# Splitting two of the down projection's seven block products a second time

## The chip, the cores and the metric

The kernel runs on one core of one Trainium2 chip. The metric is device time in microseconds (us) of one execution. Shorter is better.

## The reference

The reference mixes a sliding-window attention block `a` and a gated MLP block `b` with a sigmoid gate per token:

```
x = A_x                                     # 2048 tokens, 1024 features, bf16
g = sigmoid((x * gate_w).sum(-1))
a = attention(x @ wqkv, 32 heads, window 8, dilation 2) @ wo
b = (gelu(x @ w_gate) * (x @ w_up)) @ w_down        # 3584 hidden features
out = g * a + (1 - g) * b
```

The last step of both blocks is a matrix product, with `wo` (1024 x 1024) and with `w_down` (3584 x 1024). The kernel scales the attention output by `g` and the MLP's hidden values by `1 - g`, puts them side by side along the contraction, and so has one product for both: 2048 tokens by 4608 contracted features by 1024 outputs. That product is called `down`, and the change lies in it alone.

## The kernel before

Everything up to `down` (the gate and up products, q, k and v, the windowed softmax and the weighted sum of v) is unchanged and fills the first 522 us of the span. It leaves the hidden values in `h_d` and the attention output in `o_d`, both in device memory.

`down(s)` runs twice, for token halves `s` = 0 and 1 (1024 tokens each). In each call the left operand is cut into four blocks A11, A12, A21, A22 and the right one into R11, R12, R21, R22. The first index of an R block and the second of an A block run over the contraction (2304 features each, which are `NK` = 18 slots of 128), the others over tokens or outputs (512 each). A block is a buffer of 18 x 512 bf16 values per partition; ten such buffers, `bufs`, hold all blocks. The four output blocks are made from seven block products instead of eight, in Winograd's form of Strassen's scheme. One block product is 72 matmuls of 128 x 128 weights by 512 columns: four groups `j` of 128 tokens by 18 slots, written out by `mm`. In order they are

1. A11 x R11 into the four banks XP (its copy is kept in `u2`),
2. A12 x R21 on top of it in XP, which is output block (0, 0),
3. S x T1 into the four banks VP (copy kept in `qs`), with S = A21 + A22 and T1 = R12 - R11,
4. S x T2 into XP, with S now A21 + A22 - A11 and T2 = R22 - T1; it is added to `u2`, and that to `qs`,
5. A12 x R22 on top of VP, with A12 now A12 - S; plus `u2` it is output block (0, 1),
6. A11 x R12 into XP, with A11 now A11 - A21 and R12 now R22 - R12; plus `qs` it is output block (1, 1),
7. A22 x R21 on top of XP, with R21 now R21 - T2; plus `u2` it is output block (1, 0).

The sums and differences of blocks are VectorE's: `comb_task` makes one in five instructions over 4, 4, 4, 4 and 2 slots, `scale_task` multiplies the 14 slots of hidden values of an A block by `1 - g` in four instructions, and S - A11 goes in four pieces, one per `j`. ScalarE copies banks out. Output tiles are 128 x 512: `add_out` adds on VectorE from a bank into one of four small output tiles (`R_OUT`), and `emit` stores it, by GpSimd's DMA queue for s = 0 and by SyncE's for s = 1. The loads of the second half's blocks (`loads_1` to `loads_6`) are issued on SyncE's queue between the products of the first half.

The order on each engine is the order in which the program writes the instructions (`manual_schedule`); `take(rest, k)` writes k pieces of pending VectorE work between two groups of a product, `run(rest)` all that is left. The framework adds the semaphore waits.

Of the kernel before, what the change touches and what calls it, by code (L numbers as in the profile page):

```python
# [9 lines left out]
ALU = mybir.AluOpType  # L10
# [5 lines left out]
P = 128  # L16
SC = 512
# [37 lines left out]
R_BUF = tuple(9 + 18 * k for k in range(10))  # L55
R_U2 = 0
R_QS = 189
R_OUT = (8, 197, 198, 199)
KV = AC + HALO


# [5 lines left out]
def kernel(  # L67
# [12 lines left out]
    nc = tc.nc  # L80
    Bsz, S, D = A_x.shape
# [8 lines left out]
    NK = NPAIR + NT // 2  # L90
# [10 lines left out]
    def reg(kb, n):  # L101
        o = int(kb * KB)
        return arena[:, o:o + n]

    def reg3(kb, a, b):
        return reg(kb, a * b).rearrange("p (a b) -> p a b", a=a)
# [4 lines left out]
    def regf(kb, n):  # L111
        return reg(kb, 2 * n).bitcast(F32)

    banks = psum.tile([P, 8, SC], F32, tag="banks", bufs=1, name="banks")

    def bank(i):
        return banks[:, i, :]
# [8 lines left out]
    V = nc.vector  # L126
    TT = V.tensor_tensor

    with tc.manual_schedule(engines={mybir.EngineType.PE, mybir.EngineType.DVE, mybir.EngineType.Activation,
# [42 lines left out]
        for s in range(2):  # L172
            b0 = R_X[s]
            f = XF()
# [10 lines left out]
        def flat(a):  # L185
            return a.rearrange("p a b -> p (a b)")
# [353 lines left out]
        prod = [reg3(o, NWIN, AC) for o in pr_off]  # L540
# [210 lines left out]
        NH_ = NPAIR  # L751

        def load_A(b, s, half, c, i0, i1, with_o):
            t0 = s * SUP + c * SC
            nc.sync.dma_start(out=b[:, i0:i1, :], in_=h_src(half, t0, i0, i1))
            if with_o:
                nc.sync.dma_start(out=b[:, NH_:NK, :], in_=o_d[:, half * 4:half * 4 + 4, t0:t0 + SC])

        def h_src(half, t0, i0, i1):
            return h_d[:, :, t0:t0 + SC].rearrange("p (i two) s -> p i two s", two=2)[:, i0:i1, half, :]  # L760

        def load_R(b, half, nh):
            n0 = nh * SC
            nc.sync.dma_start(out=b[:, 0:NH_, :],
                              in_=B_w_down[:, n0:n0 + SC].rearrange("(i two p) n -> p i two n", two=2, p=P)[:, :, half, :])
            nc.sync.dma_start(out=b[:, NH_:NK, :],
                              in_=A_wo[:, n0:n0 + SC].rearrange("(p t) n -> p t n", t=NT)[:, 4 * half:4 * half + 4, :])
# [4 lines left out]
        qs = regf(R_QS, 4 * SC).rearrange("p (j n) -> p j n", j=4)  # L772
        on = [0]

        def out_tile():
            k = on[0] % 4
            on[0] += 1
            return reg(R_OUT[k], SC)

# [3 lines left out]
        def Bs(s):  # L783
            return {k: bufs[v] for k, v in plan[s].items()}

        def scale_task(b, s, c, ia, ib):
            t0 = s * SUP + c * SC
            om = omgrep[:, t0:t0 + SC].rearrange("p (o s) -> p o s", o=1)
            for i0 in range(ia, ib, 4):
                i1 = min(i0 + 4, ib)  # L790
                TT(out=b[:, i0:i1, :], in0=b[:, i0:i1, :], in1=om.to_broadcast([P, i1 - i0, SC]), op=ALU.mult)  # L791
                yield 0.05 + 0.273 * (i1 - i0)

        def comb_task(o_, a, b, op, step=4):
            for i0 in range(0, NK, step):
                i1 = min(NK, i0 + step)
                f = lambda t_: flat(t_[:, i0:i1, :])
                TT(out=f(o_), in0=f(a), in1=f(b), op=op)  # L798
                yield 0.05 + 0.273 * (i1 - i0)

        def run(*gens):
            for g in gens:
                for _ in g:
                    pass

        def pieces(*gens):
            for g in gens:
                yield from g

        def take(g, k):  # L810
            for _ in range(k):
                if next(g, None) is None:
                    break
# [19 lines left out]
        def loads_1(s):  # L833
            B = Bs(s)
            load_A(B["A11"], s, 0, 0, 0, NH_, True)
            load_R(B["R11"], 0, 0)

        def loads_2(s):
            B = Bs(s)
            load_A(B["A12"], s, 1, 0, 0, NH_, True)  # L840
            load_R(B["R21"], 1, 0)

        def loads_3(s):
            load_A(Bs(s)["A21"], s, 0, 1, 0, NH_, True)

        def loads_4(s):
            load_A(Bs(s)["A22"], s, 1, 1, 0, NH_, True)

        def loads_5(s):
            load_R(Bs(s)["R12"], 0, 1)  # L850

        def loads_6(s):
            load_R(Bs(s)["R22"], 1, 1)

        def down(s):
            B = Bs(s)
            last = s == 1
            eng = nc.sync if last else nc.gpsimd
            base = s * SUP
            XT, VT = (6, 7, 0, 1), (5, 2, 3, 4)  # L860

            def mm(ps, L, R, j, start):
                for q, i in enumerate(KORD):
                    nc.tensor.matmul(ps, lhsT=L[:, i, j * P:(j + 1) * P], rhs=R[:, i, :], start=(start and q == 0),  # L864
                                     stop=(q == NK - 1), skip_group_check=not start)

            def emit(ot, c, nh, j):
                r0 = base + c * SC + j * P
                eng.dma_start(out=o2[r0:r0 + P, nh * SC:(nh + 1) * SC], in_=ot)

            def add_out(ps, t_, c, nh, j):
                ot = out_tile()
                TT(out=ot, in0=ps, in1=t_, op=ALU.add)  # L873
                emit(ot, c, nh, j)

            A11, A12, A21, A22 = B["A11"], B["A12"], B["A21"], B["A22"]
            R11, R12, R21, R22, S, T2 = B["R11"], B["R12"], B["R21"], B["R22"], B["S"], B["T2"]
            T1 = R11
            XP = [bank(XT[j]) for j in range(4)]
            VP = [bank(VT[j]) for j in range(4)]  # L880
            rest = pieces(scale_task(A21, s, 1, 0, NH_), scale_task(A22, s, 1, 0, NH_), comb_task(S, A21, A22, ALU.add))
            for j in range(4):
                mm(XP[j], A11, R11, j, True)
                nc.scalar.copy(out=u2[:, j, :], in_=XP[j])  # L884
                yield
                take(rest, 3)
            run(rest)
            rest = comb_task(T1, R12, R11, ALU.subtract)
            for j in range(4):
                mm(XP[j], A12, R21, j, False)  # L890
                ot = out_tile()
                nc.scalar.copy(out=ot, in_=XP[j])
                emit(ot, 0, 0, j)
            run(rest)
            t2 = comb_task(T2, R22, T1, ALU.subtract)
            for j in range(4):
                mm(VP[j], S, T1, j, True)
                nc.scalar.copy(out=qs[:, j, :], in_=VP[j])
            run(t2)
            for j in range(4):  # L900
                js = slice(j * P, (j + 1) * P)
                TT(out=S[:, :, js], in0=S[:, :, js], in1=A11[:, :, js], op=ALU.subtract)  # L902
            run(comb_task(A12, A12, S, ALU.subtract), comb_task(A11, A11, A21, ALU.subtract))
            if not last:
                loads_1(1)
            rest = pieces(comb_task(R12, R22, R12, ALU.subtract), comb_task(R21, R21, T2, ALU.subtract))
            for j in range(4):
                mm(XP[j], S, T2, j, True)
                TT(out=u2[:, j, :], in0=XP[j], in1=u2[:, j, :], op=ALU.add)
                TT(out=qs[:, j, :], in0=qs[:, j, :], in1=u2[:, j, :], op=ALU.add)  # L910
                take(rest, 2)
            for j in range(4):
                mm(VP[j], A12, R22, j, False)
                add_out(VP[j], u2[:, j, :], 0, 1, j)
                take(rest, 1)
            run(rest)
            if not last:
                loads_2(1)
                loads_3(1)
                loads_5(1)  # L920
                rest = pieces(scale_task(Bs(1)["A11"], 1, 0, 0, NH_), scale_task(Bs(1)["A12"], 1, 0, 0, NH_))
            for j in range(4):
                mm(XP[j], A11, R12, j, True)
                add_out(XP[j], qs[:, j, :], 1, 1, j)
                take(rest, 1)
            if not last:
                loads_4(1)
                loads_6(1)
            for j in range(4):
                mm(XP[j], A22, R21, j, False)  # L930
                add_out(XP[j], u2[:, j, :], 1, 0, j)
                take(rest, 1)
            run(rest)

        n = len(units)
# [78 lines left out]
```

## Time and profile before

| | us |
|---|---|
| median of 3 runs | 745.09 (745.02 to 745.28) |
| the profiled execution | 744.98 |
| its span from first to last instruction | 743.2 |
| outside the span | 1.8 |

| engine | busy us | share of the span |
|---|---|---|
| TensorE (PE) | 730.6 | 98% |
| VectorE (DVE) | 594.8 | 80% |
| ScalarE (ACT) | 290.6 | 39% |
| GpSimd (POOL) | 74.4 | 10% |

A row of the profile names a line, an engine, an operation and its tiles; behind it stand how often it ran, its busy time and the mean of one. Busy times of neighbours overlap by some 0.1 us, so what a queue of equal instructions takes is read from the timeline, which merges neighbours into one row with a start and a length. The time in brackets at the end of a timeline row is the idle time of the engine before it, with what ended it. In the source of before, line 864 is the matmul of `mm`, 791 `scale_task`, 798 `comb_task`, 902 the pieces of S - A11, 909 and 910 the additions to `u2` and `qs`, 873 `add_out`, 884, 892 and 898 ScalarE's copies, 869 the stores.

### The profile page before, as it was taken

What the parts mean: (1) busy time and instruction counts of PE and PEld (TensorE: products, weight loads), DVE (VectorE), ACT (ScalarE), POOL (GpSimd) and SP (SyncE); (2) the same over time, 40 slices, a digit from 0 to 9 for tenths busy, and PEclk for the clock granted to TensorE, in tenths of its full rate; (3) what the DMA queues carried; (4) which work ended last, traced back from release to release, by engine and by line L of the source; (5) the groups of instructions that cost most, each with busy time, mean ns of one, the idle gap of its engine ahead of it and who ended that gap; (6) DMA issues with size and microseconds to landing.
All of it is one profiled execution on the core that took longest, in us unless ns stands there. A gap on an engine that the chain in (4) does not pass through costs nothing.

```text
span 743.2 us, 9134 instructions
## 1 busy us (share of the span) xinstructions
PE 730.6 (98%) x3497; PEld 356.3 (48%) x3567; DVE 594.8 (80%) x644; ACT 290.6 (39%) x498; POOL 74.4 (10%) x128
## 2 busy tenths in 40 slices
PE   8999999999999999999999999999999999999998
PEld 4465566555544444444444444444444444444443
DVE  3958888967999999999999999984487954936921
ACT  4454445535466655555555555555111000110000
POOL 1011111221201010101010010000010021000000
PEclk9999999999999999999999999999999999999999
DMA  9960000272323625535345644447990799400011
GB/s 279 267 202 24 19 15 22 75 227 95 106 81 108 194 77 185 181 104 160 128 142 171 212 145 142 154 159 264 291 307 1 246 360 359 138 28 1 9 42 36
DMA packets 107213, 106.95 MB, mean 144 GB/s; under 512 B 16656, under 2 KB 94480, under 8 KB 107168
## 3 DMA queue, kind: packets, MB, share of 16 engines
q1 hardware_dynamic: 97856, 77.41, 34.0%
q0 software_dynamic: 9024, 28.42, 11.4%
q8 instruction: 28, 0.46, 0.2%
q10 hardware_dynamic: 288, 0.52, 0.2%
q14 instruction: 17, 0.14, 0.1%
HBM read 73.73 MB, written 30.51 MB: 140 GB/s over the span
## 4 chain that ended last, share of the span: by engine, by line
PE 68%; issue 12%; DVE 4%; POOL 1%; DMA 1%; ACT 0%; DVEq 0%; POOLq 0%
PE banks L329 38%; PE banks L864 29%; PE banks L565 1%; DVE arena L366 1%; DVE arena L285 1%; POOL h_d L247 1%; DVE arena L560 1%; DVE arena L607 0%; DMA h_d<-arena 0%; DMA arena<-h_d 0%; POOL o_d L710 0%; DVE arena L246 0%; DVE md L633 0%; ACT L641 0%; DVE md L644 0%
## 5 line engine op out<-in xcount | busy, mean ns | idle before, releaser
L329 PE MATMUL banks<-arena 128*128 128x512 bf16 x2135 | 474.1, 379 | 4.2 <-DVE arena L366 1.3
L329 PEld LDWEIGHTS <-arena 128*128 128x128 bf16 x2184 | 239.9, 111 | 236.9 <-issue 11.1
L864 PE MATMUL banks<-arena 128*128 128x512 bf16 x989 | 217.1, 379 | 1.9 <-DVE arena L791 0.9
L864 PEld LDWEIGHTS <-arena 128*128 128x128 bf16 x1008 | 98.6, 98 | 120.0 <-DVE arena L791 1.3
L366 DVE TENSOR_TENSOR arena<-banks,arena 128x1024 bf16<-128x1024 f32 x78 | 95.2, 1221 | 45.9 <-PE banks L329 27.4
L352 ACT COPY arena<-banks 128x512 f32<-128x512 f32 x78 | 45.7, 586 | 130.2 <-PE banks L329 130.2
L683 DVE TENSOR_TENSOR arena<-arena 128x2048 bf16<-128x2048 bf16 x64 | 77.0, 1220 | 0.4
L337 ACT CAST arena<-banks 128x512 bf16<-128x512 f32 x102 | 59.7, 585 | 44.6 <-PE banks L329 44.3
L560 DVE TENSOR_TENSOR arena<-arena 128x2048 bf16<-128x2048 bf16 x64 | 75.2, 1219 | 0.3
L690 DVE TENSOR_TENSOR arena<-arena 128x2048 bf16<-128x2048 bf16 (+2 forms) x96 | 73.8, 776 | 1.0
L798 DVE TENSOR_TENSOR arena<-arena 128x2048 bf16<-128x2048 bf16 (+1 forms) x70 | 73.3, 1111 | 0.1
L873 DVE TENSOR_TENSOR arena<-banks,arena 128x512 bf16<-128x512 f32 x24 | 16.6, 690 | 47.0 <-PE banks L864 41.7
L359 ACT COPY banks<-banks 128x512 f32<-128x512 f32 x78 | 44.5, 571 | 21.7 <-PE banks L329 19.8
L347 ACT COPY banks<-banks 128x512 f32<-128x512 f32 x78 | 45.0, 577 | 14.2 <-PE banks L329 13.4
L247 POOL DMA_DIRECT2D h_d<-arena x28 | 20.0, 715 | 288.6 <-DVE arena L246 275.3
L791 DVE TENSOR_TENSOR arena<-arena,omgrep 128x2048 bf16<-128x2048 bf16 (+1 forms) x32 | 33.2, 1085 | 11.3 <-DMA arena<-h_d 11.2
L884 ACT COPY arena<-banks 128x512 f32<-128x512 f32 x8 | 4.7, 586 | 90.3 <-PE banks L864 90.3
L285 DVE TENSOR_TENSOR arena<-arena 128x1024 bf16<-128x1024 bf16 x60 | 38.6, 685 | 0.5
L335 ACT ACTIVATE arena<-banks 128x512 bf16<-128x512 f32 x54 | 32.2, 597 | 15.3 <-PE banks L329 15.2
L246 DVE TENSOR_TENSOR arena<-arena 128x2048 bf16<-128x2048 bf16 x28 | 34.1, 1216 | 1.7 <-ACT arena L337 1.5
L374 ACT ACTIVATE arena<-arena 128x1024 bf16<-128x1024 bf16 x27 | 28.3, 1048 | 0.0
L902 DVE TENSOR_TENSOR arena<-arena 128x2304 bf16<-128x2304 bf16 x8 | 10.8, 1357 | 21.7 <-PE banks L864 21.7
(68 smaller groups left out, 245.6 us busy)
## 6 DMA issues: line engine op xcount, KB each, us to landing
h_d<-arena POOLq DMA_DIRECT2D x28, 512.0 KB, 4.1
arena<-in_B_w_down_dram SPq DMA_DIRECT2D x8, 1792.0 KB, 13.2
arena<-h_d SPq DMA_DIRECT2D x6, 1792.0 KB, 13.6
arena<-in_B_w_gate_dram SPq DMA_DIRECT2D x15, 512.0 KB, 5.2
arena<-in_B_w_up_dram SPq DMA_DIRECT2D x15, 512.0 KB, 4.4
arena<-in_A_wqkv_dram SPq DMA_DIRECT2D x6, 1024.0 KB, 10.3
arena<-v_d SPq DMA_DIRECT2D x8, 544.0 KB, 6.3
v_d<-arena POOLq DMA_DIRECT2D x16, 256.0 KB, 2.3
```

Of the source, the lines that this page charges most:

```text
L285: TT(out=o_, in0=a, in1=b_, op=op)
L329: self.pe = nc.tensor.matmul(ps, lhsT=self.L[form](kt), rhs=rhs[:, kt, :], start=(start and kt == 0), stop=(kt == HK - 1), skip_group_chec ...
L337: nc.scalar.copy(out=o_, in_=i_)
L347: nc.scalar.copy(out=self.Y, in_=self.X)
L352: nc.scalar.copy(out=self.p5s, in_=self.V)
L359: nc.scalar.copy(out=self.Z, in_=self.Y)
L366: TT(out=self.T[:, :, c2s], in0=pair, in1=self.p5s.rearrange("p (o n) -> p o n", o=1).to_broadcast([P, 2, SC]), op=ALU.add)
L560: TT(out=dst, in0=q.rearrange("p (o s) -> p o s", o=1).to_broadcast([P, NWIN, AC]), in1=_win_ap(k, [[-DIL, NWIN], [1, AC]]), op=ALU.mult)
L683: TT(out=prod2[(t // 2) % 2][:, t % 2], in0=ab, in1=_win_ap(v[:, t, HALO:HALO + AC], [[SJ, NJ], [-DIL, NWIN], [1, SJ]]), op=ALU.mult)
L690: TT(out=out_, in0=h(0), in1=h(1), op=ALU.add)
L798: TT(out=f(o_), in0=f(a), in1=f(b), op=op)
L864: nc.tensor.matmul(ps, lhsT=L[:, i, j * P:(j + 1) * P], rhs=R[:, i, :], start=(start and q == 0), stop=(q == NK - 1), skip_group_check=not ...
```

## The change

Products 4 (S x T2) and 6 (A11 x R12) are each cut once more by the same scheme (`level2`). A block becomes four quarters of 9 slots by 256 columns (`quarter`), and the product seven inner ones, each of 2 groups by 9 slots of matmuls with 256 columns, 18 in all. `forms_L` and `forms_R` make the four quarter forms that each operand needs on VectorE, one instruction of 2304 elements each. The inner sums stay in the two halves of the four XP banks: VectorE zeroes the left halves (`zero_left`), ScalarE copies half banks into one another between the inner products, and two VectorE instructions add the copy `p5d` of the third inner product at the end.

The quarter forms need room. `LF` lies in the buffer of R11, `RF2` in that of A22, `RF7` in that of S. So A22 is loaded and scaled a second time for product 7. The copy `p5d` takes two of the four output tiles, which leaves two. Several steps move: R12 becomes R22 - R12 ahead of T2 instead of during product 4; A12 - S and A11 - A21 are no longer written together; `woven` alternates the left and right forms during product 5; R21 - T2 and A22's second scaling follow `level2` of product 6, and the four `add_out` of product 6 follow them; the second half's loads are written in another order, and the scaling of its A12 moves from product 6 of the first half to product 1 of the second.

```diff
@@ -55,7 +55,8 @@
 R_BUF = tuple(9 + 18 * k for k in range(10))
 R_U2 = 0
 R_QS = 189
-R_OUT = (8, 197, 198, 199)
+R_OUT = (8, 197)
+R_P5D = 198
 KV = AC + HALO
 
 
@@ -773,7 +774,7 @@
         on = [0]
 
         def out_tile():
-            k = on[0] % 4
+            k = on[0] % 2
             on[0] += 1
             return reg(R_OUT[k], SC)
 
@@ -852,6 +853,61 @@
         def loads_6(s):
             load_R(Bs(s)["R22"], 1, 1)
 
+        KH, HN = NK // 2, SC // 2
+        p5d = regf(R_P5D, SC).rearrange("p (j n) -> p j n", j=2)
+
+        def quarter(b, kh, h):
+            return b[:, kh * KH:(kh + 1) * KH, h * HN:(h + 1) * HN]
+
+        def quads(b):
+            return b.rearrange("p k n -> p (k n)").rearrange("p (f k n) -> p f k n", f=4, k=KH)
+
+        def forms_L(f, b):
+            q = lambda kh, h: quarter(b, kh, h)
+            for o_, a, b_, op in ((f[:, 0], q(0, 1), q(1, 1), ALU.add), (f[:, 1], f[:, 0], q(0, 0), ALU.subtract),
+                                  (f[:, 2], q(0, 0), q(0, 1), ALU.subtract), (f[:, 3], q(1, 0), f[:, 1], ALU.subtract)):
+                TT(out=o_, in0=a, in1=b_, op=op)
+                yield 1.3
+
+        def forms_R(f, b):
+            q = lambda kh, h: quarter(b, kh, h)
+            for o_, a, b_, op in ((f[:, 0], q(0, 1), q(0, 0), ALU.subtract), (f[:, 1], q(1, 1), f[:, 0], ALU.subtract),
+                                  (f[:, 2], q(1, 1), q(0, 1), ALU.subtract), (f[:, 3], q(1, 0), f[:, 1], ALU.subtract)):
+                TT(out=o_, in0=a, in1=b_, op=op)
+                yield 1.3
+
+        def woven(*gens):
+            for cs in zip(*gens):
+                yield from cs
+
+        def zero_left(b0, b1):
+            for b in (b0, b1):
+                V.memset(banks[:, b:b + 2, 0:HN], 0.0)
+
+        def level2(b0, b1, L, R, lf, rf):
+            lq, rq = lambda r, c: quarter(L, c, r), lambda r, c: quarter(R, r, c)
+            c = lambda i, h, j: banks[:, (b0, b1)[i] + j, h * HN:(h + 1) * HN]
+            both = lambda i, h: banks[:, (b0, b1)[i]:(b0, b1)[i] + 2, h * HN:(h + 1) * HN]
+
+            def prod(i, h, l, r, then=None):
+                for j in range(2):
+                    for kt in range(KH):
+                        nc.tensor.matmul(c(i, h, j), lhsT=l[:, kt, j * P:(j + 1) * P], rhs=r[:, kt, :], start=False,
+                                         stop=(kt == KH - 1), skip_group_check=True)
+                    if then:
+                        then(j)
+
+            cp = lambda d, s_: nc.scalar.copy(out=d, in_=s_)
+            prod(0, 0, lq(0, 0), rq(0, 0), lambda j: cp(c(1, 1, j), c(0, 0, j)))
+            prod(0, 0, lq(0, 1), rq(1, 0))
+            prod(1, 0, lf[:, 0], rf[:, 0], lambda j: cp(p5d[:, j, :], c(1, 0, j)))
+            prod(1, 1, lf[:, 1], rf[:, 1], lambda j: cp(c(0, 1, j), c(1, 1, j)))
+            prod(1, 1, lf[:, 2], rf[:, 2], lambda j: cp(c(1, 0, j), c(1, 1, j)))
+            prod(0, 1, lf[:, 3], rq(1, 1))
+            TT(out=both(1, 1), in0=both(1, 1), in1=p5d, op=ALU.add)
+            prod(1, 0, lq(1, 1), rf[:, 3])
+            TT(out=both(0, 1), in0=both(0, 1), in1=p5d, op=ALU.add)
+
         def down(s):
             B = Bs(s)
             last = s == 1
@@ -878,54 +934,61 @@
             T1 = R11
             XP = [bank(XT[j]) for j in range(4)]
             VP = [bank(VT[j]) for j in range(4)]
-            rest = pieces(scale_task(A21, s, 1, 0, NH_), scale_task(A22, s, 1, 0, NH_), comb_task(S, A21, A22, ALU.add))
+            LF, RF2, RF7 = quads(R11), quads(A22), quads(S)
+            rest = pieces(scale_task(A12, s, 0, 0, NH_) if last else (), scale_task(A21, s, 1, 0, NH_),
+                          scale_task(A22, s, 1, 0, NH_), comb_task(S, A21, A22, ALU.add))
             for j in range(4):
                 mm(XP[j], A11, R11, j, True)
                 nc.scalar.copy(out=u2[:, j, :], in_=XP[j])
                 yield
                 take(rest, 3)
             run(rest)
-            rest = comb_task(T1, R12, R11, ALU.subtract)
             for j in range(4):
                 mm(XP[j], A12, R21, j, False)
                 ot = out_tile()
                 nc.scalar.copy(out=ot, in_=XP[j])
                 emit(ot, 0, 0, j)
-            run(rest)
-            t2 = comb_task(T2, R22, T1, ALU.subtract)
+            run(comb_task(T1, R12, R11, ALU.subtract), comb_task(R12, R22, R12, ALU.subtract))
             for j in range(4):
                 mm(VP[j], S, T1, j, True)
                 nc.scalar.copy(out=qs[:, j, :], in_=VP[j])
-            run(t2)
+            run(comb_task(T2, R22, T1, ALU.subtract))
+            zero_left(XT[0], XT[2])
+            run(forms_R(RF2, T2))
             for j in range(4):
                 js = slice(j * P, (j + 1) * P)
                 TT(out=S[:, :, js], in0=S[:, :, js], in1=A11[:, :, js], op=ALU.subtract)
-            run(comb_task(A12, A12, S, ALU.subtract), comb_task(A11, A11, A21, ALU.subtract))
-            if not last:
-                loads_1(1)
-            rest = pieces(comb_task(R12, R22, R12, ALU.subtract), comb_task(R21, R21, T2, ALU.subtract))
+            run(forms_L(LF, S), comb_task(A12, A12, S, ALU.subtract))
+            level2(XT[0], XT[2], S, T2, LF, RF2)
+            load_A(A22, s, 1, 1, 0, NH_, True)
             for j in range(4):
-                mm(XP[j], S, T2, j, True)
                 TT(out=u2[:, j, :], in0=XP[j], in1=u2[:, j, :], op=ALU.add)
                 TT(out=qs[:, j, :], in0=qs[:, j, :], in1=u2[:, j, :], op=ALU.add)
-                take(rest, 2)
+            zero_left(XT[0], XT[2])
+            run(comb_task(A11, A11, A21, ALU.subtract))
+            if not last:
+                load_A(Bs(1)["A11"], 1, 0, 0, 0, NH_, True)
+            rest = woven(forms_L(LF, A11), forms_R(RF7, R12))
             for j in range(4):
                 mm(VP[j], A12, R22, j, False)
                 add_out(VP[j], u2[:, j, :], 0, 1, j)
-                take(rest, 1)
+                if j > 0:
+                    take(rest, 2)
+            if not last:
+                loads_3(1)
+                loads_5(1)
+            run(rest)
+            level2(XT[0], XT[2], A11, R12, LF, RF7)
+            rest = pieces(scale_task(A22, s, 1, 0, NH_), comb_task(R21, R21, T2, ALU.subtract))
             run(rest)
             if not last:
+                load_R(Bs(1)["R11"], 0, 0)
                 loads_2(1)
-                loads_3(1)
-                loads_5(1)
-                rest = pieces(scale_task(Bs(1)["A11"], 1, 0, 0, NH_), scale_task(Bs(1)["A12"], 1, 0, 0, NH_))
-            for j in range(4):
-                mm(XP[j], A11, R12, j, True)
-                add_out(XP[j], qs[:, j, :], 1, 1, j)
-                take(rest, 1)
-            if not last:
                 loads_4(1)
                 loads_6(1)
+                rest = scale_task(Bs(1)["A11"], 1, 0, 0, NH_)
+            for j in range(4):
+                add_out(XP[j], qs[:, j, :], 1, 1, j)
             for j in range(4):
                 mm(XP[j], A22, R21, j, False)
                 add_out(XP[j], u2[:, j, :], 1, 0, j)
```

## The prediction

> **What bounds the kernel now.** I read the engines' shares first, then the chain of waits over the last 200 us, then the timeline of each engine through `down`.
>
> The chain over 545 to 744 us says whose work sets the end there:
>
> ```profile
> by line: PE banks L864 97.5%; issue 0.5%; DVE arena L873 0.3%
> ```
>
> PE's timeline over the same stretch is one row, with no idle time inside it:
>
> ```profile
> 554.79 184.92 PE L864 MATMUL banks<-arena 128*128 128x512 bf16 x839
> ```
>
> So in `down` before, only PE counts. In ScalarE's timeline the four groups of a product follow each other every 3.885 us (copies at 634.85, 638.74, 642.62), so a matmul takes 3.885 / 18 = 0.2158 us and a product 15.54. DVE is the engine that the change loads. Its timeline:
>
> ```profile
> 545.55 15.51 DVE L798 TENSOR_TENSOR arena<-arena 128x2048 bf16<-128x2048 bf16 x15
> 560.98 2.62 DVE L902 TENSOR_TENSOR arena<-arena 128x2304 bf16<-128x2304 bf16 x2
> ...
> 568.81 1.36 DVE L902 TENSOR_TENSOR arena<-arena 128x2304 bf16<-128x2304 bf16 x1 [2.52 <-PE banks L864]
> ...
> 592.35 2.35 DVE L798 TENSOR_TENSOR arena<-arena 128x2048 bf16<-128x2048 bf16 x2
> ```
>
> The first row is three block sums, S, T1 and T2, at 5.14 us each. In the first half they run late: T2 ends at 561.0 while product 3 is on PE until 568.8. Later DVE waits for PE; before, it is never in PE's way. Prices by shape:
>
> ```profile
> L902 DVE TENSOR_TENSOR arena<-arena 128x2304 bf16<-128x2304 bf16 x8 | 10.8, 1357 | 21.7 <-PE banks L864 21.7
> L909 DVE TENSOR_TENSOR arena<-banks,arena 128x512 f32<-128x512 f32 x8 | 5.5, 684 | 0.0
> L548 DVE MEMSET arena<- 128x256 uint32 x1 | 0.3, 272 | 0.0
> out_dram<-arena POOLq DMA_DIRECT2D x16, 128.0 KB, 5.3
> ```
>
> The last is the time from issue to landing of a store in the first half, where loads fill the DMA engines.
>
> **What the shorter products save.** A 256-column matmul does not occur before. The neighbours are in PE's first microseconds:
>
> ```profile
> 1.20 2.74 PE L143 MATMUL banks<-arena 128*128 128x512 bf16 x6 [1.20 <-DVE arena L140]
> 4.38 1.07 PE L205 MATMUL banks<-ident,arena 128*128 128x128 bf16 x16 [0.44 <-DMA arena<-in_A_x_dram]
> ```
>
> Sixteen of 128 columns, each with its own weights, start 0.0557 us apart once in step, so weight loading is hidden even there. A line through 0.0557 at 128 and 0.2158 at 512 gives 0.1091 at 256; the bounds are half of the large one, 0.1079, and twice the small one, 0.1114. Seven inner products of 18 are 126 x 0.1091 = 13.75 us against 15.54: 1.79 saved each, 7.2 over four.
>
> **What DVE has to do for it.** Per product eight quarter forms of 2304 elements, at the pitch of L902 (1.26, and about 0.13 more where one reads the one before): 5.2 us for each side. A zeroing of 512 words is 0.49 by the slope of the SBUF memsets (112 ns at 64 words, 272 at 256), 0.69 by an addition on a bank; I take 0.55, for the SBUF rows are the same operation: 1.1 for two. An addition of `p5d` is 0.61 at its pitch. A22's second scaling is 4.0 (four at 1.14 and 0.60). ScalarE's half copies, under the 0.57 of a full one, each have a group of 9 matmuls (0.98) on PE to hide in.
>
> **First half, product 4.** DVE: S and T1 end at 555.8, R12's difference now goes ahead of T2 (561.0), T2 566.1, two zeroings 567.2, right forms 572.5, S - A11 in four pieces to 577.6. Before, these pieces followed product 3's groups as they ended; now they start 3.7 us after its last. PE has finished product 3 at 568.8 and can only start on the first piece, at 573.9: 5 us idle. DVE goes on: left forms 582.9, A12 - S 588.1, addition of `p5d` 588.8. In the order of the built program the seventh inner product waits for that addition, which stands behind A12 - S in DVE's queue. It runs 588.9 to 590.9. Product 4 thus ends 22.1 us after product 3: **+6.5**.
>
> **First half, products 5 and 6.** Product 5 has A12 and takes its 15.54, to 606.4. DVE meanwhile does the second `p5d` addition, `u2` and `qs` (5.9), zeroings, A11 - A21 (601.6), four `add_out` and eight forms (2 x 5.2), with one wait: two output tiles are left, and a third `add_out` waits 5.3 us for the first store. The forms end at 616.5; each is there 0.3 us or more before its inner product. Product 6 runs 606.4 to 620.2: **-1.8**.
>
> **First half, product 7.** Here is the largest term. Behind inner product 6 (ends 618.2; the seventh, 1.96, is all that PE still has) DVE does in a row: second `p5d` addition to 619.0, A22's scaling 4.0, R21 - T2 5.14, and the first `add_out`, 0.61 and 0.2 to its end, which must read bank XP[0] before product 7 adds to it. That is 629.1; PE was free at 620.2: **+8.9**. Before, R21 - T2 was written among the groups of products 4 and 5, and each `add_out` between two groups of product 6. A22's reload is not in it: issued at 591 with no other load on the queue, it lands some 9 us later (the first load of before, issued at 580.0, landed at 587.9 and 589.4).
>
> **Second half.** Product 1 needs A11 scaled; the third scaling piece stands behind a third `add_out` that waits 5.3 us for a store: 648.1, needed at 646.2: **+2.0**. The loads, about 7.3 us a block in before's landings, end near 661; R22 is first read at 672. DVE then has T1 done 6 us ahead of product 3 and is in step with PE: product 4 starts on time and only waits for the `p5d` addition behind left forms and A12 - S, 14.8 us: **-0.7**. Product 6 **-1.8**, product 7 the same queue as before it, **+8.9**. SyncE's stores stand behind A22's reload, which waits for product 4 only; nothing there is late.
>
> Sum without the next term: 6.5 - 1.8 + 8.9 + 2.0 - 0.7 - 1.8 + 8.9 = +22.0, so 744.98 + 22.0 = 767.0.
>
> **PE's clock after a gap.** The six matmuls of L143 above start 0.426 us apart (2.74 less the last one's 0.61, over 5), half rate, and the trace's clock record goes to full 3.1 us after the first of them. The same record goes to half 5.3 us after PE's last matmul. Gaps of 8.9 us are longer than that. A restart then does half work for 3.1 us and loses about 1.6 to 1.7. After the first half's product 7 it takes the place of product 1's wait for A11, of which 0.3 is left; after the second half's it counts in full: 22.0 - 1.7 + 1.7 + 1.7 = **+23.7**. The gap of 5.0 us is on the edge, and there DVE sets the pace whatever PE's rate.
>
> The Trainium skill, "TensorE: Matmul & The Clock Gate", section "HAM oscillation — how this bites in real kernels", advises against idle gaps of PE over about 3.4 us, because the clock falls back to half. No row before the end shows PE idle longer than 1.2 us, so this trace cannot confirm where in a kernel that happens; by that rule the 5 us gap would restart at half rate as well.
>
> **Rivals.**
> 1. The clock stays full through gaps of 9 us: 767.0. For it: no gap of that kind inside the trace. Against: the record after the last matmul.
> 2. Faster: DVE's queue hides. Then the four shorter products give 4 x 1.79 and the kernel takes 737.8. It decides at product 7: the work on DVE between inner product 6 and the first `add_out` would have to fit into the 1.96 us of inner product 7. For it: DVE is 80% busy only. Against: the queue is in order and that work is 10.5 us by rows of the same shapes.
> 3. The matmuls do not become half as long: the rows have 98 ns for a weight load, and if it showed, a matmul would take 0.108 + 0.098 = 0.206 and a product 26.0 us, 10.4 more than before: 4 x 10.4 and the gaps that stay (5.0 ahead of product 4, twice 7.2 ahead of product 7) are +61, 806. Against: the transposes' 0.0557.
> 4. Quarter forms at half DVE's rate (some 2.45 each, for their runs are 256 long): 32 forms x 1.2 = 38 us more, some 35 of it ahead of PE, with the 22 about +57, 802. Against: L902 writes runs of 128 at 0.59 ns per element, like the dense 2048 at 0.60.
>
> **How the numbers follow.** Forecast (stalls with restarts at half rate) 0.66; rival 1 0.22; rival 2 0.02; rivals 3 and 4 0.05 together; the rest, 0.05, is slips of the queue beyond these rows. The time is 744.98 + 23.7 = 768.7; the median of before is 0.1 above the profiled run, which I leave in the rounding. Low end: no restarts and stores at 3.1 us (the quickest in before) +20.0, so 765, and 1 below for waits that I count too long. High end: matmuls at 0.1114 (504 of them, of which DVE's pace covers about half), forms at the full 1.357 (16 of the 32 ahead of PE) and half rate for twice 3.1 us after the two gaps add 0.6, 1.6 and 2.9: 773.8, and 1 for waits counted too short: 775. A measurement of this kernel can tell some 0.2% (1.5 us) from no change; only rival 2 is on the other side of it.
>
> **What would show it.** Right: PE idle 8 to 10 us ahead of product 7's first matmul in both halves, ended by DVE's `add_out`; 4 to 6 us ahead of the first half's product 4, ended by a piece of S - A11; 256-column matmuls some 0.109 us apart; product 7's first matmuls 0.43 us apart. Wrong: PE continuous through product 7, a pitch over 0.12, quarter forms over 1.5 us, or PE waiting for a load.

## The result, and the profile after

| | before | after |
|---|---|---|
| median, us | 745.02 | 770.93 |
| range of 5 runs, us | 744.72 to 745.28 | 769.55 to 771.95 |
| the profiled execution, us | 744.98 | 769.55 |
| its span, us | 743.2 | 767.8 |

The changed kernel takes 1.0347 times as long, with a 95% interval of 1.0332 to 1.0362. The forecast was 768.7 (764 to 775). The profiled execution is the quickest of the five after; sums below go against its 769.55.

The chain of waits over 545 to 768 us answers to the one row that gave PE (TensorE) 97.5% before. Now PE has 41% and the rows of VectorE (DVE) 11% together. The 41.7% under "issue" say little: nearly all of it stands between GpSimd's stores before 641 us, where the chain follows the stores and not PE:

```profile
by line: issue 41.7%; PE banks L920 34.8%; PE banks L895 6.2%; DVE arena L799 4.6%; DMA out_dram<-arena 2.7%; POOL out_dram L925 2.7%; DVE arena L869 2.4%; DVE arena L792 2.3%; DVE arena L929 0.9%; DVE arena L960 0.6%; DVE banks L907 0.3%; 
```

PE's timeline was one row from 554.79 on. It now breaks at six waits of over half a microsecond. In the source of after, L920 is the matmul of `mm`, L895 that of `level2`, L960 the pieces of S - A11, L907 and L909 the `p5d` additions, L929 `add_out`, L792 the scaling, L799 the block sums of `comb_task`, L869 and L876 the left and right quarter forms, L885 the zeroing, L900 ScalarE's half copies and L925 the stores. In the runs with four output tiles below, these numbers are two higher (L897 is `level2`, L922 `mm`, L931 `add_out`, L871 the left forms).

```profile
572.00 13.67 PE L895 MATMUL banks<-arena 128*128 128x256 bf16 x108 [3.13 <-DVE arena L960]
586.88 2.13 PE L895 MATMUL banks<-arena 128*128 128x256 bf16 x18 [1.21 <-DVE banks L907]
...
627.52 0.58 PE L920 MATMUL banks<-arena 128*128 128x512 bf16 x1 [8.57 <-DVE arena L929]
...
648.85 45.07 PE L920 MATMUL banks<-arena 128*128 128x512 bf16 x204 [2.28 <-DVE arena L792]
...
746.43 0.58 PE L920 MATMUL banks<-arena 128*128 128x512 bf16 x1 [8.57 <-DVE arena L929]
```

The waits are the ones that the forecast named, each with its releaser: product 4 of the first half on S - A11, its seventh inner product on `p5d` (0.74 us in the second half, the row not shown), product 7 of both halves on the first `add_out` of product 6, product 1 of the second half on the scaled A11.

VectorE's timeline ahead of product 7 shows the queue as it was summed: the second `p5d` addition, A22's second scaling, R21 - T2 and the first `add_out`:

```profile
617.03 0.70 DVE L909 TENSOR_TENSOR banks<-banks,arena 128x512 f32<-128x512 f32 x1 [0.82 <-PE banks L895]
617.64 4.09 DVE L792 TENSOR_TENSOR arena<-arena,omgrep 128x2048 bf16<-128x2048 bf16 x4
621.64 5.23 DVE L799 TENSOR_TENSOR arena<-arena 128x2048 bf16<-128x2048 bf16 x5
626.78 1.29 DVE L929 TENSOR_TENSOR arena<-banks,arena 128x512 bf16<-128x512 f32 x2
```

And the granted clock (the column after the five engines' busy times: 0.67 and 0.50 of full speed) in two 9 us windows at the gaps ahead of product 7:

```profile
621.00:630.00 9.00, 2.25 (x5) 0.84 (x6) 7.07 (x9) 0.00 (x0) 1.08 (x2) 0.67 1.10 348
740.00:749.00 9.00, 2.35 (x6) 0.90 (x7) 7.73 (x11) 0.00 (x0) 0.00 (x0) 0.50 0.09 29
```

### The profile page after: what moved, and what is told of

It reads as the page before. It is cut to its first block, busy times and chain, and to the rows that moved or that the text cites. A ratio compares the mean times of both kernels' runs of the same rounds, so it can differ in the third digit from the quotient of the medians.

```text
span 767.8 us, 9679 instructions
## 1 busy us (share of the span) xinstructions
PE 730.5 (95%) x3717; PEld 379.5 (49%) x3783; DVE 651.7 (85%) x700; ACT 302.7 (39%) x530; POOL 74.7 (10%) x128
## 4 chain that ended last, share of the span: by engine, by line
PE 51%; issue 26%; DVE 5%; POOL 2%; DMA 1%; ACT 0%; POOLq 0%; DVEq 0%
PE banks L330 38%; PE banks L920 10%; PE banks L895 2%; DVE arena L799 1%; PE banks L566 1%; POOL out_dram L925 1%; POOL h_d L248 1%; DMA out_dram<-arena 1%; DVE arena L869 1%; DVE arena L792 1%; DVE arena L367 1%; DMA arena<-in_B_w_up_dram 0%; POOL o_d L711 0%; DVE arena L286 0%; DVE arena L561 0%
## 5 line engine op out<-in xcount | busy, mean ns | idle before, releaser
L330 PE MATMUL banks<-arena 128*128 128x512 bf16 x2135 | 474.1, 379 | 4.2 <-DVE arena L367 1.3
L330 PEld LDWEIGHTS <-arena 128*128 128x128 bf16 x2184 | 239.9, 111 | 237.0 <-issue 11.1
L920 PE MATMUL banks<-arena 128*128 128x512 bf16 x705 | 159.1, 384 | 21.4 <-DVE arena L929 17.1
L920 PEld LDWEIGHTS <-arena 128*128 128x128 bf16 x720 | 71.1, 99 | 107.9 <-issue 21.8
L353 ACT COPY arena<-banks 128x512 f32<-128x512 f32 x78 | 45.8, 587 | 130.1 <-PE banks L330 130.1
L799 DVE TENSOR_TENSOR arena<-arena 128x2048 bf16<-128x2048 bf16 (+1 forms) x70 | 72.7, 1116 | 0.0
L895 PE MATMUL banks<-arena 128*128 128x256 bf16 x504 | 57.9, 277 | 5.6 <-DVE arena L960 3.1
L895 PEld LDWEIGHTS <-arena 128*128 128x128 bf16 x504 | 49.7, 99 | 14.1 <-DVE arena L960 4.0
L792 DVE TENSOR_TENSOR arena<-arena,omgrep 128x2048 bf16<-128x2048 bf16 (+1 forms) x40 | 41.1, 1087 | 9.3 <-DMA arena<-h_d 9.2
L929 DVE TENSOR_TENSOR arena<-banks,arena 128x512 bf16<-128x512 f32 x24 | 16.1, 689 | 31.3 <-PE banks L920 17.7
L900 ACT COPY banks<-banks 128x256 f32<-128x256 f32 x24 | 8.6, 357 | 61.0 <-PE banks L895 61.0
```

What stands on the lines that cost most here:

```text
L330: self.pe = nc.tensor.matmul(ps, lhsT=self.L[form](kt), rhs=rhs[:, kt, :], start=(start and kt == 0), stop=(kt == HK - 1), skip_group_chec ...
L353: nc.scalar.copy(out=self.p5s, in_=self.V)
L895: nc.tensor.matmul(c(i, h, j), lhsT=l[:, kt, j * P:(j + 1) * P], rhs=r[:, kt, :], start=False, stop=(kt == KH - 1), skip_group_check=True)
```

## The experiments

Each run has its own runs of the kernel before beside it (745.0 to 745.4 us in median). Times are medians.

**Product 6 alone split.** The order of before is kept for product 4, A22 and R21 - T2:

```diff
-            level2(XT[0], XT[2], S, T2, LF, RF2)
-            load_A(A22, s, 1, 1, 0, NH_, True)
+            rest = comb_task(R21, R21, T2, ALU.subtract)
             for j in range(4):
+                mm(XP[j], S, T2, j, True)
...
-            rest = pieces(scale_task(A22, s, 1, 0, NH_), comb_task(R21, R21, T2, ALU.subtract))
-            run(rest)
```

> Product 6 alone is split; product 4 is one plain product again, A22 is not overwritten, loaded or scaled again, and R21 - T2 goes back among the groups of product 4. Theory (DVE's queue: with both products split, VectorE has more to do behind inner product 6 than PE has left to do): here VectorE's forms fit beside product 5, nothing but two p5d additions stands behind inner product 6, and PE has no gap ahead of product 7; each half gains about 1.8 us less some 1.4 us of waiting for the scaled A11 in the second half's product 1 (two output tiles): 745.0 - 2.2 = 742.8 us. Rival (the split itself costs: half-bank copies, zeroing and hand-overs between 18-matmul products are dearer than the matmuls saved): half of the splits cost about half of the loss, 745 + 13 = 758 us.

Measured: 747.34 us, ratio 1.0032 (1.0019 to 1.0044). The split itself makes no gap: none stands ahead of product 7 in either half. But the expected 742.8 was missed by 4.5, most of it in one place:

```profile
600.15 13.92 PE L895 MATMUL banks<-arena 128*128 128x256 bf16 x126
613.90 17.43 PE L920 MATMUL banks<-arena 128*128 128x512 bf16 x78
634.94 77.70 PE L920 MATMUL banks<-arena 128*128 128x512 bf16 x345 [3.61 <-DVE arena L792]
```

Product 6 takes 613.90 - 600.15 = 13.75 us, as forecast. Product 1 of the second half then waits 3.6 us for the scaled A11 (1.4 expected), and the clock record has half rate for 3.41 us from 634.71, which costs about 1.6 more (half of the 3.18 us of it in which PE worked). VectorE's timeline shows what held the scaling up:

```profile
620.02 1.44 DVE L929 TENSOR_TENSOR arena<-banks,arena 128x512 bf16<-128x512 f32 x2 [5.86 <-DMA out_dram<-arena]
626.55 0.69 DVE L929 TENSOR_TENSOR arena<-banks,arena 128x512 bf16<-128x512 f32 x1 [5.08 <-DMA out_dram<-arena]
...
633.06 0.69 DVE L929 TENSOR_TENSOR arena<-banks,arena 128x512 bf16<-128x512 f32 x1 [2.96 <-DMA out_dram<-arena]
633.67 1.22 DVE L792 TENSOR_TENSOR arena<-arena,omgrep 128x2048 bf16<-128x2048 bf16 x1
```

Three times an `add_out` waits for a store to free one of two output tiles, and the scaling pieces stand behind them.

**Product 4 alone split.** Product 6 is plain; A22's second scaling and R21 - T2 go among product 5's groups:

```diff
-            rest = woven(forms_L(LF, A11), forms_R(RF7, R12))
+            rest = pieces(comb_task(R21, R21, T2, ALU.subtract), scale_task(A22, s, 1, 0, NH_))
...
-            level2(XT[0], XT[2], A11, R12, LF, RF7)
...
+                mm(XP[j], A11, R12, j, True)
```

> Product 4 alone is split; product 6 is one plain product, with A22's second scaling and R21 - T2 written among the groups of product 5. Theory (VectorE's queue): the first half's product 4 still starts late and waits for the p5d addition, +4.6 as measured in the changed kernel (+6.5 by the forecast's sum), the second half's gives -0.7 to +1, and no gap stands ahead of product 7: 745 + 4 to 8 = 749 to 753 us. Rival (the split itself costs the same wherever it stands): about half the loss, 758 us.

Measured: 754.10 us, ratio 1.0119 (1.0103 to 1.0134), 1 us above the expected 749 to 753 and 4 below the rival's 758. Nothing waits ahead of product 7. In the first half product 4 starts 5.0 us late; in the second it has three short waits, 3.7 together. PE was not held up ahead of product 7 there and is through with product 3 at 684.6, where the changed kernel is at 693.8, so VectorE is the late one:

```profile
574.40 14.59 PE L895 MATMUL banks<-arena 128*128 128x256 bf16 x108 [5.03 <-DVE arena L960]
...
685.85 4.39 PE L895 MATMUL banks<-arena 128*128 128x256 bf16 x36 [1.22 <-DVE arena L960]
691.05 8.03 PE L895 MATMUL banks<-arena 128*128 128x256 bf16 x72 [0.81 <-DVE arena L869]
700.73 2.13 PE L895 MATMUL banks<-arena 128*128 128x256 bf16 x18 [1.64 <-DVE banks L907]
```

Both splits alone cost 2.2 + 8.9 us by the medians, 11.1; together they cost 25.9. The two gaps ahead of product 7 belong to neither alone.

**A22's second scaling left out.**

```diff
-            rest = pieces(scale_task(A22, s, 1, 0, NH_), comb_task(R21, R21, T2, ALU.subtract))
+            rest = comb_task(R21, R21, T2, ALU.subtract)
```

> The changed kernel without the second scaling of A22 ahead of product 7 (its reload stays): this part of the computation is left out, so A22's hidden values go into product 7 unscaled. Theory (VectorE's queue): PE's gap ahead of product 7 shrinks by the 4.0 us of the four scalings, from 8.6 to about 4.6 in each half, and with it most of the half-rate restart: 771 - 8 to -11 = 760 to 763 us. Rival (the gap is the hand-over of half-written banks or the reload's landing): the gap stays 8.6 and the time 770 to 771 us.

Measured: 763.07 us, ratio 1.0239 (1.0225 to 1.0253), 7.9 under the changed kernel. The gap shrank by just the four scalings, 8.57 to 4.56 in the first half and 4.55 in the second, which is shown:

```profile
740.69 0.59 PE L920 MATMUL banks<-arena 128*128 128x512 bf16 x1 [4.55 <-DVE arena L929]
741.50 17.36 PE L920 MATMUL banks<-arena 128*128 128x512 bf16 x69 [0.22 <-issue]
```

So the gap is VectorE's queue. What did not come is that a shorter gap would spare the half rate: product 7 still takes 740.69 to 758.70 (its last row's end less the 0.16 by which a matmul's row outlasts the 0.216 from one start to the next), 18.0 us against 15.54.

**The same work in another place.** R21 - T2 goes ahead of product 6's `p5d` additions:

```diff
+            run(comb_task(R21, R21, T2, ALU.subtract))
             level2(XT[0], XT[2], A11, R12, LF, RF7)
-            rest = pieces(scale_task(A22, s, 1, 0, NH_), comb_task(R21, R21, T2, ALU.subtract))
+            rest = scale_task(A22, s, 1, 0, NH_)
```

> The changed kernel with R21 - T2 (5.2 us of VectorE) written ahead of product 6's p5d additions instead of behind them: the same work, another place. If the order of VectorE's queue alone makes the gap ahead of product 7, it shrinks by 5.2 us in both halves and nothing else grows: 770.9 - 10.4 and less half rate, 757 to 760 us. If VectorE is also full (it has 3.2 us idle there in the second half, none in the first), a part comes back as a new wait ahead of inner product 7: some 2 us in the second half, some 4 us in the first, so 761 to 765 us. If the gap has to do with the banks and not with VectorE's queue: 771 us.

Measured: 765.16 us, ratio 1.0265 (1.0251 to 1.0279), 0.2 above the 761 to 765 expected of a full VectorE. In the first half the wait mostly changes its place, in the second about half of it is gone:

```profile
623.72 3.74 PE L895 MATMUL banks<-arena 128*128 128x256 bf16 x18 [4.18 <-DVE banks L907]
628.92 17.43 PE L920 MATMUL banks<-arena 128*128 128x512 bf16 x80 [1.46 <-DVE arena L929]
...
737.99 2.12 PE L895 MATMUL banks<-arena 128*128 128x256 bf16 x18 [1.12 <-DVE banks L907]
743.19 17.39 PE L920 MATMUL banks<-arena 128*128 128x512 bf16 x72 [3.07 <-DVE arena L929]
```

So the order of VectorE's queue is a part of the loss and the volume of its work another: 5.6 us of waiting are left in the first half and 4.2 in the second, of 8.6 each.

**Four output tiles.** Two small buffers of the softmax, no longer read by then, are the other two:

```diff
-            k = on[0] % 2
+            k = on[0] % 4
             on[0] += 1
+            if k > 1:
+                return (md[:].rearrange("p a s -> p (a s)").bitcast(BF16), gblk[:].rearrange("p a s -> p (a s)"))[k - 2]
```

> The changed kernel with four output tiles again (two small buffers of the softmax, unused by then, serve as the other two). Theory: the two-tile limit costs the wait of the first half's product 5 (3.6 us of VectorE) and, through the late scaling of A11, 2.3 us of PE in the second half's product 1; the gap of 8.6 us ahead of product 7 stays. 770.9 - 2.3 - about 0.5 (product 6's short wait) = 768 us. Rival (store landings don't matter, product 1's wait comes from the loads): 770.9 us.

Measured: 767.67 us, ratio 1.0302 (1.0288 to 1.0317), 3.3 us under the changed kernel. From product 7 of the first half to product 4 of the second PE has one row, so product 1 no longer waits, and the gaps stay:

```profile
626.91 65.01 PE L922 MATMUL banks<-arena 128*128 128x512 bf16 x288 [8.56 <-DVE arena L931]
```

**The gap filled.** PE gets 38 more matmuls behind product 6 in each half; they add nothing to the outputs:

```diff
             level2(XT[0], XT[2], A11, R12, LF, RF7)
+            for q in range(38):
+                nc.tensor.matmul(VP[3], lhsT=R12[:, q % 8, 0:P], rhs=R12[:, q % 8, :], start=True, stop=True)
```

> The changed kernel with 38 extra 512-column matmuls behind product 6 of each half, into a bank that nothing reads again before it is rewritten, so that PE is busy (8.2 us) while it would wait for product 7's operands. Clock theory: PE's granted clock stays full through that stretch, product 7's first matmuls start 0.216 us apart instead of 0.43, and the time falls by about 1.9 us for the second half and by 0 to 1.9 for the first (there product 1's wait for the scaled A11 can take it back): 767 to 769 us. Rival (the granted clock follows something else than PE's idleness, or the half rate is hidden behind VectorE's queue): 770 to 771.5 us.

Measured: 770.92 us, the same as the changed kernel; the expected 767 to 769 was missed. In the second half the clock theory holds: from product 6's start to PE's end it takes 726.45 to 764.47, 38.0 us, where the changed kernel took 723.94 to 763.87, 39.9. The first half gave it back: product 1's wait for A11 grew to 0.60 + 3.75 us, and behind that the record has half rate for 3.41 us. With two output tiles this run could not decide, so the fill was repeated with four:

> Four output tiles and the 38 extra matmuls in the gap ahead of product 7 of each half: the first half's saving can no longer be taken back by product 1's wait for the scaled A11. Clock theory: against the run with four tiles (767.7 us) both restarts at half rate go, 1.9 us each: 763.9 us. Rival (the half rate costs nothing on the path, or comes back elsewhere): 767.7 us.

Measured: 764.46 us, ratio 1.0261 (1.0247 to 1.0275), 3.2 under the 767.67 of four tiles without the fill. The granted clock is full where the changed kernel had 0.67 and 0.50:

```profile
621.00:630.00 9.00, 8.64 (x41) 3.81 (x39) 8.20 (x11) 0.00 (x0) 2.12 (x4) 1.00 1.10 348
740.00:749.00 9.00, 8.64 (x41) 3.84 (x40) 4.72 (x7) 0.00 (x0) 0.00 (x0) 1.00 0.23 75
```

The two restarts cost 1.6 us each, by the difference of the medians. In the two profiled executions the fill shortens product 7 by more, 2.7 us in the first half and 2.0 in the second.

**Product 6 alone, with four output tiles.** The two edits above together.

> Product 6 alone split, as in the run before, and four output tiles. Theory: the run with product 6 alone lost 3.6 us of waiting for the scaled A11, and the restart at half rate behind it, to the two-tile limit; without it the split of product 6 gives its 2 x 1.79 us: 745.1 - 3.6 = 741.5 us. Rival (the wait is the loads' new order): 747 us as there.

Measured: 741.94 us, ratio 0.9955 (0.9941 to 0.9968): faster than before by 3.5 us, the 2 x 1.79 of the forecast's first term.

```profile
599.50 13.92 PE L897 MATMUL banks<-arena 128*128 128x256 bf16 x126
613.25 93.40 PE L922 MATMUL banks<-arena 128*128 128x512 bf16 x432
706.49 13.92 PE L897 MATMUL banks<-arena 128*128 128x256 bf16 x126
```

**Three splits.** To the last run, product 4's split is added in the second half alone, and its right forms lie in A21's buffer, so A22 is not overwritten. These are the main lines; the whole edit also moves R21 - T2 ahead of product 6's `p5d` additions in that half, puts a part of A12 - S inside product 4 and changes the order of some loads:

```diff
-            LF, RF2, RF7 = quads(R11), quads(A22), quads(S)
+            LF, RF2, RF7 = quads(R11), quads(A21), quads(S)
...
+            if last:
+                run(comb_task(A11, A11, A21, ALU.subtract))
...
-                TT(out=S[:, :, js], in0=S[:, :, js], in1=A11[:, :, js], op=ALU.subtract)
+                TT(out=S[:, :, js], in0=(A22 if last else S)[:, :, js], in1=A11[:, :, js], op=ALU.subtract)
```

> Product 6 split in both halves, product 4 in the second half alone, four output tiles; product 4's right forms lie in A21's buffer (A11 - A21 is made before, and S - A11 becomes A22 - A11), so A22 is neither loaded nor scaled twice, and R21 - T2 stands ahead of product 6's additions. Theory (VectorE's volume): the second half's queue is full up to product 4, which starts 0.4 us late and waits once for 1 us, so the third split brings almost nothing beyond the two: 741 to 742.5 us. If only order and the second scaling were the fault: 745.1 - 3 x 1.79 = 739.7 us.

Measured: 741.35 us, ratio 0.9948 (0.9936 to 0.9961), the quickest version here and 29.6 us under the changed kernel. Its interval overlaps with that of two splits, and so do the spans (739.3 to 740.1 us, and 739.4 to 740.2 there): the third split brings at most little. Product 4 waits for its forms once:

```profile
676.26 4.39 PE L897 MATMUL banks<-arena 128*128 128x256 bf16 x36
681.45 10.07 PE L897 MATMUL banks<-arena 128*128 128x256 bf16 x90 [0.81 <-DVE arena L871]
```

## Why the prediction was right, point by point

The forecast's terms beside what the profile after shows. A product is taken from its first matmul to the next product's first, or to its last row's end less 0.16:

| term | forecast, us | measured, us | from |
|---|---|---|---|
| first half, product 4 | +6.5 | +4.6 | 568.71 to 588.84, less 15.54 |
| product 6 | -1.8 | -1.1 | 604.38 to 618.80; one wait of 0.48 |
| ahead of product 7 | +8.9 | +8.7 | 618.80 to 627.52 |
| half rate in product 7 | +1.7 | +1.6 | 627.52 to 644.68 |
| second half, product 1 | +0.3 | +2.4 | 646.41 to 648.85 |
| product 4 | -0.7 | -0.9 | 693.75 to 708.40 |
| product 6 | -1.8 | -1.8 | 723.94 to 737.69 |
| ahead of product 7 | +8.9 | +8.7 | 737.69 to 746.43 |
| half rate in product 7 | +1.7 | +1.9 | 746.43 to 763.87 |
| sum | +23.7 | +24.1 | |

The other 0.5 of the 24.6 us between the two executions lies outside these products.

The steps came as forecast, but the nearness of the two sums is in part luck. Two terms are off by about 2 us each, product 4 of the first half and product 1 of the second, and they cancel. By the medians the change is +25.9, 2.2 more than forecast. And one of the signs did not come: the wait ahead of the first half's product 4 is 3.1 us, where 4 to 6 were named.

**Prices.** The matmul of 256 columns starts every 0.109 us in the raw trace, the forecast's 0.1091, and its weights hide; rival 3 fell here. The zeroing is 0.485 us, the end that the slope gave and not the 0.55 taken. The quarter forms take 1.354, as L902 did before; rival 4 fell.

```profile
L876 DVE TENSOR_TENSOR arena<-arena 128x2304 bf16<-128x2304 bf16 x16 | 21.3, 1354 | 0.1
L885 DVE MEMSET banks<- 128x512 f32 x8 | 3.9, 485 | 0.6
L900 ACT COPY banks<-banks 128x256 f32<-128x256 f32 x24 | 8.6, 357 | 61.0 <-PE banks L895 61.0
```

**Product 4 of the first half** came out 1.9 us below its term. VectorE's chain there begins with A22's load, which landed at 539.67 in this execution and at 541.51 in the one before; nothing ahead of it was changed. Over the runs with this chain unchanged the wait went with the landing: 3.1 to 3.6 us where it came at 539.7 to 539.8, 3.7 at 540.3, 4.9 to 6.0 where it came at 541.1 to 541.2 (in two of these three T1 waited 0.8 and 1.1 us for another load as well). The term was read from one execution as if it were fixed. Product 6 of that half, which PE reached 2.0 us early, waited 0.48 for a form that the forecast had ready 0.3 ahead.

**Product 1 of the second half** is the step that was mis-sized. It was put at +2.0 without restarts, of which the half rate in product 7 was to take all but 0.3. Measured, it is 2.4 beside the 1.6 of half rate, 4.1 without restarts. The wait ends with a chain on VectorE: three rounds, in each of which an `add_out` fills a tile, its store lands and the next `add_out` may use the tile; then comes the third scaling piece. The first `add_out` is the one at 626.78 that releases product 7, the next three are

```profile
633.28 0.69 DVE L929 TENSOR_TENSOR arena<-banks,arena 128x512 bf16<-128x512 f32 x1 [5.21 <-PE banks L920]
...
639.80 0.69 DVE L929 TENSOR_TENSOR arena<-banks,arena 128x512 bf16<-128x512 f32 x1 [4.97 <-DMA out_dram<-arena]
...
646.97 0.69 DVE L929 TENSOR_TENSOR arena<-banks,arena 128x512 bf16<-128x512 f32 x1 [3.61 <-DMA out_dram<-arena]
647.58 1.22 DVE L792 TENSOR_TENSOR arena<-arena,omgrep 128x2048 bf16<-128x2048 bf16 x1
```

The profile puts the first of these down to PE, but the tile's store landed at 633.16, just before it. Chain and PE start from the same `add_out`, so product 7's start, 1.6 us earlier than forecast, moves both and leaves the wait as it is. Too short in the sum was the chain: from product 7's first matmul to the scaled A11 it had 629.1 to 648.1, 19.0 us, and 627.52 to 648.85 is 21.3. Worked back, its 648.1 comes out with rounds of 6.0, the store's 5.3 and the 0.69 of the addition. A measured round is 6.5 with a store of 5.4: some 0.3 pass from the addition to the store's issue and 0.1 from the landing to the next addition. One of the three stores took 6.1. With product 6 alone split the same chain takes 21.0 us (613.90 to 634.94) though it starts 14 us earlier, and in the other runs with product 6 split and two tiles 20.9 to 22.1; that is why that run missed its 742.8. Four tiles (-3.3 us) confirm that the tiles set it. The step said rightly that stores set this time; it left out the hand-overs between the rounds.

**The clock.** Rival 1, a clock that stays full, is refuted: 0.67 and 0.50 in the windows, and 3.2 us come back when the gaps are filled. The advice of the Trainium skill that the prediction cited ("TensorE: Matmul & The Clock Gate", section "HAM oscillation — how this bites in real kernels"), no idle gap of PE over about 3.4 us, agrees with the half rate behind the gaps of 8.6. As a sharp limit it does not agree: half rate came behind the 3.1 us ahead of product 4 too (the record falls at 572.80, 0.8 us after PE had resumed at 572.00), and it did not come behind one wait of 3.5 us in another run. That the forecast's 1.7 a restart met 1.6 and 1.9 is in part luck: 3.3 and 3.9 us of half rate were left when PE resumed, and with four tiles, behind the same gaps, it was 5.5 and 4.0.

**Rival 2**, a queue that hides, does hold with product 6 alone and four output tiles: 741.94. What decides is what stands behind inner product 6. With product 4 split too, that is R21 - T2 and a scaling that only exists because A22's buffer was taken.

## What to carry to other kernels

When PE is 98% busy, a scheme with fewer matmuls has to be paid for on another engine: sum that engine's queue product by product, above all what stands between the last inner result and the next product's first operand. Borrowed buffers cost more than their space: taking A22's made a second scaling in the worst place, and taking two output tiles put three rounds of addition and store ahead of an operand. A chain that goes through stores is priced by whole rounds, hand-overs with it. Splitting the one product whose forms fit beside other work won 3.5 us with four output tiles; splitting two, as the change does, lost 26.

## What the runs showed of the hardware

- Half rate comes in whole periods. In the trace's clock record every stretch at half rate between PE's first microseconds and its last matmul is 3.41, 6.83 or 10.24 us long, once, twice or three times 3.41. That fits the Trainium skill, "TensorE: Matmul & The Clock Gate", section "What's actually happening", which has a free-running window of 3413 ns.
- The same idle time can end either way: a wait of 3.1 us met half rate and one of 3.5 us (the run with R21 - T2 earlier, ahead of 649.82) did not. Of the eight waits of PE of 3.1 to 3.8 us in these runs it was the only one that did not; none of 2.4 us or less did, and all of 4.2 us or more did. That the window's phase decides is the reading that fits; no run set the phase.
- A longer gap does not mean a dearer restart. Behind gaps of 8.6 us product 7 lost 1.6 and 1.9 us in the changed kernel and 2.7 and 2.0 with four tiles; in the second half behind the gap cut to 4.6 us it lost 2.5. Each loss is about half of the half-rate time that was left when PE resumed: 3.3, 3.9, 5.5, 4.0 and 5.0 us.
- VectorE's zeroing of the left halves of two banks (512 words) takes 0.485 us, what the slope of the SBUF memsets gives (0.49), and a ScalarE copy of 256 columns between banks 0.357 us; the kernel before has neither.
